# A token MLP in which every product reads the two halves of its columns in turn

## The chip, the cores and the metric

The kernel runs on one core of one Trainium2 chip. The metric is the device time of one execution in microseconds. Three executions of the kernel before gave 1683.47, 1689.55 and 1690.23 us; their median, 1689.55 us, is the number that a changed kernel is held against.

## The reference

Two stages. The first is a long convolution along the sequence, with a filter made from a small MLP of position embeddings; the second is an MLP over all 24,960 tokens.

```python
def _attn_ref(x, v, pos_emb, w1, w2):            # x, v: 2 x 12480 x 128
    h_filt = (np.maximum(pos_emb @ w1, 0.0) @ w2) * np.exp(-0.01 * pos)[:, None]
    u = x * v
    y = irfft(rfft(u, n=2 * S) * rfft(h_filt, n=2 * S)[None])[:, :S]   # along the sequence
    return x * y

def _moe_ref(x, w_in, w_out):                    # x: 24960 x 128, w_in: 128 x 2048
    h = x @ w_in
    return np.maximum(0.01 * h, h) @ w_out       # w_out: 2048 x 128
```

## The kernel before, in words

The convolution is done as matrix products with the factors of a transform, in four steps with two trips through DRAM. Batch 0 goes through its first three steps ahead of the MLP; batch 1 and the last step of both run inside the MLP's loop, cut into pieces by hand.

The MLP holds tokens along the columns. The 24,960 columns are cut into 50 tiles: one of 390, 46 of 512, one of 314 and two of 352 (`widths`). For each tile k and each of 16 slices f of the 2048 hidden channels, `m1(k, f)` makes 128 hidden channels and `m2(k, f, r)` adds their share to the output. Numbers are split into a high and a low part of the type float32r (`zh`, `zl` for the input; `rh`, `rl` for the hidden values; `w_in_h`, `w_in_l`, `w_out_h`, `w_out_l` for the weights), and each product is three matmuls, high by high, high by low, low by high. In each of them the 128x128 piece of the weights stands in the array, and the tile of `zh`, `zl`, `rh` or `rl`, up to 512 columns long, moves through it. So a step (k, f) is six matmuls: three into a PSUM tile `mh` (line 977), three that add to the PSUM tile `acc` of the tile k (lines 1010 to 1012).

Between the two, the hidden values are taken out of `mh`. There are two ways. Where `sums(k)` holds (21 of the 50 tiles, all in the first half), ScalarE writes `rh` as the positive part of `mh` (line 981) and VectorE writes `rl` as what is left of it, reading `mh` too (line 982); the linear part of the activation then enters through three extra matmuls per tile with a product matrix `wc` (lines 1006 to 1008). In the other 29 tiles ScalarE reads `mh` once and writes `r` (line 990), and `rh` and `rl` are made from `r` in SBUF: `rh` by ScalarE for even f (line 994), by VectorE for odd f (line 992), `rl` by VectorE (line 995).

The order is written out by hand in the last loop of the kernel: `m1` of a step, then `m2` of the step three steps before (`DEEP` is 3), then whatever pieces of convolution, loads and the output stage are due at that step. `mh` has three PSUM buffers, `rh` and `rl` have five SBUF buffers each, and there are two `acc` tiles, used in turn.

When a tile is done, `finish(k)` copies `acc` to SBUF tiles `ot` of 390 columns each (line 1025, ScalarE); TensorE transposes each `ot`, and it goes out.

Of the kernel before, what the change touches and what calls it, by code (L numbers as in the profile page):

```python
# [12 lines left out]
AF = mybir.ActivationFunctionType  # L13
ALU = mybir.AluOpType
# [16 lines left out]
def tile_conv_mlp(ctx, tc, x, v, pos_emb, w1, w2, w_in, w_out, cf, cr, cg, cb, ci, cw, out):  # L31
    nc = tc.nc
# [78 lines left out]
    def run(g):  # L111
        for _ in g:
            pass


    def chunk(c):
        k0 = c * KC
        return k0, min(KC, NA - k0)
# [36 lines left out]
    def back(dp, parts, c):  # L155

        for s in range(2):
            for j, w in halves(c):
                three(dp[s][:, w], (mi_h[j][:, s], mi_l[j][:, s]), (parts[0][:, s, w], parts[1][:, s, w]))

    def turned(pool, psum, m2, m1):

        ph = pool.tile([128, 2, KH + 1], F32, tag="ph0", name="ph0", bufs=1)
# [50 lines left out]
    with tc.manual_schedule():  # L214
# [22 lines left out]
        with ExitStack() as st:  # L237
# [86 lines left out]
            for c in range(NC0):  # L324
# [52 lines left out]
                for mm in range(MC):  # L377
                    a = psa.tile([NA, 2, 512], F32, tag="a", name="a", bufs=3)
# [193 lines left out]
        ld, cin, z, acc = {}, {}, {}, {}  # L572
# [103 lines left out]
        with ExitStack() as st:  # L676
# [73 lines left out]
            def two(tag):  # L750
                return [psb.tile([128, 512], F32, tag=tag, name=tag + "p", bufs=2) for _ in range(2)]
# [41 lines left out]
            for i, c in enumerate(ORD):  # L793
# [16 lines left out]
                n = chunk(c)[1]  # L810
                t, es = bins.pop(c), eh.pop(c)
                hp = two("h")
                for ri in range(2):
                    for k in range(n):
                        h, j = 64 * (k % 2), ri * n // 2 + k // 2
# [53 lines left out]
        widths = [TOK] + [WIDE] * ((S - TOK) // WIDE) + [rest]  # L869
# [9 lines left out]
        def sums(k):  # L879
            return at0[k] < S and k not in OWN and k < LAST  # L880

        def pieces_of(t):

            for k in range(NTL):
                lo, hi = max(at0[k], t * TOK), min(at0[k + 1], t * TOK + TOK)
                if lo < hi:
                    yield k, lo - at0[k], lo - t * TOK, hi - lo
# [81 lines left out]

        def m1(k, f):  # L970
            w = widths[k]
            zh, zl = (i[:, :w] for i in z[k])
            hp = ps.tile([128, WIDE], F32, tag="mh", name="mh", bufs=3)[:, :w]
            fs = slice(f * 128, f * 128 + 128)
            for i, (u, m) in enumerate(((w_in_h, zh), (w_in_l, zh), (w_in_h, zl)) if k == f == 0 else
                                       ((w_in_h, zh), (w_in_h, zl), (w_in_l, zh))):
                nc.tensor.matmul(hp, u[:, fs], m, start=(i == 0), stop=(i == 2))  # L977
            rh = sm.tile([128, WIDE], F32R, tag="rh", name="rh", bufs=DEEP + 2)[:, :w]
            rl = sm.tile([128, WIDE], F32R, tag="rl", name="rl", bufs=DEEP + 2)[:, :w]
            if sums(k):  # L980
                nc.scalar.activation(out=rh, in_=hp, func=AF.Relu)  # L981
                nc.vector.scalar_tensor_tensor(out=rl, in0=hp, scalar=0.0, in1=rh, op0=ALU.max, op1=ALU.subtract)  # L982
            else:
                tag, pool, bufs = ((("th", psc["pool"], 1), ("tl", psc["pool"], 1), ("ct1", psc["pool"], 1),
                                    ("ph", psc["pool"], 1), ("pl", psc["pool"], 1)) if k in OWN else
                                   (("s1", s0, 3), ("hd", psc["pool"], 2), ("ct1", psc["pool"], 1),
                                    ("s1", s0, 3), ("hd", psc["pool"], 2)))[f % 5]
                r = pool.tile([128, 2048 if tag == "hd" else 1024], F32R if tag in ("th", "tl", "ph", "pl") else F32,
                              tag=tag, name="r", bufs=bufs)[:, :w].bitcast(F32)
                nc.scalar.activation(out=r, in_=hp, func=AF.Lrelu, alpha=0.01)  # L990
                if f % 2:
                    nc.vector.tensor_copy(rh, r)  # L992
                else:
                    nc.scalar.copy(rh, r)  # L994
                nc.vector.tensor_tensor(out=rl, in0=r, in1=rh, op=ALU.subtract)  # L995
            return rh, rl

        def m2(k, f, r):
            rh, rl = r
            w = widths[k]  # L1000
            if f == 0:
                acc[k] = ps.tile([128, WIDE], F32, tag=f"acc{k % 2}", name="acc", bufs=1)
            if f == 0 and sums(k):
                zh, zl = (i[:, :w] for i in z[k])
                ap = acc[k][:, :w]
                nc.tensor.matmul(ap, wc_h, zh, start=True, stop=False)
                nc.tensor.matmul(ap, wc_h, zl, start=False, stop=False)
                nc.tensor.matmul(ap, wc_l, zh, start=False, stop=False)
            ap = acc[k][:, :w]
            nc.tensor.matmul(ap, w_out_h[:, f, :], rh, start=(f == 0 and not sums(k)), stop=False)  # L1010
            nc.tensor.matmul(ap, w_out_h[:, f, :], rl, start=False, stop=False)  # L1011
            nc.tensor.matmul(ap, w_out_l[:, f, :], rh, start=False, stop=(f == NF - 1))  # L1012

        ots = {}

        def finish(k):

            ap = acc.pop(k)
            whole = []
            for t in range(at0[k] // TOK, (at0[k + 1] - 1) // TOK + 1):  # L1020
                for kk, a, c, n in pieces_of(t):
                    if kk == k:
                        if t not in ots:
                            ots[t] = sm.tile([128, TOK], F32, tag="ot", name="ot", bufs=3)
                        nc.scalar.copy(ots[t][:, c:c + n], ap[:, a:a + n])
                        if c + n == TOK:
                            whole.append(t)
            for t in whole:
                yield
                b, mp = divmod(t, NT)  # L1030
                ot = ots.pop(t)
                end = t == total - 1
                op = ps.tile([NA, 4, D], F32, tag="io", name="op")
                op0 = ps.tile([128, WIDE], F32, tag="cv", name="op0", bufs=2)[:NA].rearrange(
                    "a (q d) -> a q d", d=D) if end else op
                for p, m, at, n in COLS:
                    nc.tensor.transpose((op if p else op0)[:, 2 * p + m, :], ot[:, at:at + NA], ident)  # L1037
                os_ = sm.tile([NA, 2, 2, D], F32, tag="os", name="os")
                n = b * S
                dst = out[n:n + ROWS * NB, :].rearrange("(a p n) d -> a p n d", p=2, n=HB)  # L1040
                r0 = n + ROWS * NB + 2 * mp
                if end:
                    nc.scalar.copy(os_[:, 1], op[:, 2:4])
                    nc.vector.tensor_copy(os_[:, 0], op0[:, 0:2])
                    for eng, p in ((nc.scalar, 1), (nc.sync, 0)):
                        eng.dma_start(out=dst[:R0, p, 2 * mp:2 * mp + 2, :], in_=os_[:R0, p])
                    nc.scalar.dma_start(out=dst[R0:, :, 2 * mp:2 * mp + 2, :], in_=os_[R0:ROWS])
                    nc.sync.dma_start(out=out[None, r0:r0 + 2, :], in_=os_[ROWS:, 0])
                    return
                nc.scalar.copy(os_.rearrange("a p m d -> a (p m) d"), op)  # L1050
                yield
                for r in (slice(0, R0), slice(R0, ROWS)):
                    nc.sync.dma_start(out=dst[r, :, 2 * mp:2 * mp + 2, :], in_=os_[r])
                nc.sync.dma_start(out=out[None, r0:r0 + 2, :], in_=os_[ROWS:, 0])
# [34 lines left out]
        for t in range(1, total):  # L1089
            g, p = turn_at[t], turn_at.get(t - 1, 0)  # L1090
            if t in leads:
                lo = max(g - 19, p + 2, gets[t] + 7)
                till = ends[t - 1] if t - 1 in second and g - ends[t - 1] < 8 else g - 2
                hi = max((lo + till) // 2, gets[t + 1] + 7)
# [3 lines left out]
            elif t in gets and t not in second:  # L1098
                lo = max(g - 9, p + 1, gets[t] + 5)
# [85 lines left out]
        for k in range(NTL):  # L1185
            for f in range(NF):
                i = k * NF + f
                pend.append((k, f, m1(k, f)))
                if len(pend) > DEEP:
                    m2(*pend.pop(0))  # L1190
                for s_ in steps.get(i, ()):
                    do(*s_, i)
                if f == DEEP - 1 and k:
                    fin = finish(k - 1)
                if f >= DEEP - 1 and (f - DEEP + 1) % 2 == 0:
                    next(fin, None)
                if i < SLOTS:
                    while done < min(pieces, pace(i)):
                        next(conv, None)
                        done += 1  # L1200
        for q in pend:
            m2(*q)
        run(finish(NTL - 1))


# [66 lines left out]
```

## Time and profile before

| what | us |
|---|---|
| median of three runs | 1689.55 |
| the profiled execution, its own time | 1684.68 |
| its span, first to last instruction | 1682.9 |
| TensorE busy within the span | 1628.1 |
| VectorE busy | 1193.9 |
| ScalarE busy | 1008.0 |
| GpSimd busy | 821.6 |

The profile is of one execution. A busy time says how long an engine had an instruction in work; it is an average over stages. Matmuls overlap at their ends, so the time that a matmul takes on its row is longer than the distance from its start to the start of the next, and it is the distance that counts for the sum. The MLP begins at 337 us and runs to the end.

### The profile page before, as it was taken

Reading aid. Unit: us, or ns where it says so; the run is one execution under the profiler, and the core shown is the slowest. Engines: PE = TensorE matmul, PEld = TensorE weight load, DVE = VectorE, ACT = ScalarE, POOL = GpSimd, SP = SyncE. Lnnn points to the kernel's source line nnn. Section 1 sums busy time; section 2 is a strip of 40 time slices with the busy share of each in tenths; the row PEclk is TensorE's granted clock in tenths of the full one; section 3 lists DMA queues with packets and bytes.
Section 4 is the critical chain, followed back from the end, with each engine's and each line's share of the span. In section 5 each row is a group of like instructions: output and inputs, shape, how many; then the busy total and the mean of one; then the engine's idle time right before and its main releaser. Section 6 shows DMA issues by size and latency. Waiting matters only on the chain.

```text
span 1682.9 us, 27337 instructions
## 1 busy us (share of the span) xinstructions
PE 1628.1 (97%) x9173; PEld 1319.2 (78%) x9173; DVE 1193.9 (71%) x1785; ACT 1008.0 (60%) x2056; POOL 821.6 (49%) x804
## 2 busy tenths in 40 slices
PE   6897999899999999999999999999999999999999
PEld 6786555488888888888888888888888888887888
DVE  4775888656775566666566664887887887878765
ACT  1332454345654577676677676666667676676666
POOL 3563212245643376767567763654464545445410
PEclk9998999999999999999999999999999999999999
DMA  8898999766766466656566631321212212121100
GB/s 237 285 301 248 342 321 342 253 195 186 209 177 196 124 170 196 192 157 171 155 177 165 167 105 55 122 68 56 61 61 66 75 53 75 56 61 56 56 11 20
DMA packets 166357, 253.30 MB, mean 151 GB/s; under 512 B 14302, under 2 KB 119026, under 8 KB 163146
## 3 DMA queue, kind: packets, MB, share of 16 engines
q1 hardware_dynamic: 146478, 226.29, 45.6%
q10 hardware_dynamic: 19740, 25.28, 4.3%
q8 instruction: 73, 1.20, 0.3%
q14 instruction: 66, 0.54, 0.1%
HBM read 168.00 MB, written 83.43 MB: 149 GB/s over the span
## 4 chain that ended last, share of the span: by engine, by line
PE 79%; DVE 9%; DMA 7%; issue 2%; ACT 1%; SPq 1%; POOL 0%; ACTq 0%; DVEq 0%; POOLq 0%
PE mh L977 30%; PE acc L1011 10%; PE acc L1012 10%; PE acc L1010 10%; PE cv L138 4%; PE yp L903 4%; PE cv L425 3%; DMA scr<-o 2%; DMA ft<-in_cf_dram 2%; PE op L1037 2%; PE zp L922 1%; PE up L124 1%; DVE rl L995 1%; DVE ta L132 1%; PE a L381 1%
## 5 line engine op out<-in xcount | busy, mean ns | idle before, releaser
L995 DVE TENSOR_TENSOR rl<-r,rh 128x512 fp32r<-128x512 f32 (+2 forms) x464 | 398.1, 875 | 101.0 <-ACT rh L994 92.4
L990 ACT ACTIVATE r<-mh 128x512 f32<-128x512 f32 (+2 forms) x464 | 271.3, 586 | 193.8 <-PE mh L977 175.2
L982 DVE SCALAR_TENSOR_TENSOR rl<-mh,rh 128x512 fp32r<-128x512 f32 (+1 forms) x336 | 227.8, 683 | 222.9 <-ACT rh L981 220.6
L977 PE MATMUL mh<-zh,w_in_h 128*128 128x512 f32 (+3 forms) x800 | 327.6, 410 | 0.8 <-ACT zh L966 0.7
L1011 PE MATMUL acc<-rl,w_out_h 128*128 128x512 f32 (+3 forms) x800 | 309.6, 387 | 1.3 <-DVE rl L995 0.6
L977 PE MATMUL mh<-zh,w_in_l 128*128 128x512 f32 (+3 forms) x800 | 310.3, 388 | 0.0
L1010 PE MATMUL acc<-rh,w_out_h 128*128 128x512 f32 (+3 forms) x800 | 310.3, 388 | 0.0
L1012 PE MATMUL acc<-rh,w_out_l 128*128 128x512 f32 (+3 forms) x800 | 309.9, 387 | 0.0
L977 PE MATMUL mh<-zl,w_in_h 128*128 128x512 f32 (+3 forms) x800 | 309.4, 387 | 0.0
L981 ACT ACTIVATE rh<-mh 128x512 fp32r<-128x512 f32 (+1 forms) x336 | 199.7, 596 | 157.3 <-PE mh L977 151.4
L936 POOL TENSOR_TENSOR zl<-zf,zh 128x390 fp32r<-128x390 f32 (+24 forms) x110 | 69.3, 643 | 406.1 <-ACT zh L935 401.0
L666 POOL TENSOR_TENSOR cp<-cq,cp 98x256 f32<-98x256 f32 x248 | 223.0, 899 | 34.4 <-DVE cp L654 17.7
L992 DVE CAST rh<-r 128x512 fp32r<-128x512 f32 (+2 forms) x232 | 146.5, 632 | 48.6 <-ACT r L990 47.3
L1011 PEld LDWEIGHTS acc<-rl,w_out_h 128*128 128x128 f32 x800 | 150.3, 188 | 38.5 <-DVE rl L995 7.0
L977 PEld LDWEIGHTS mh<-zh,w_in_l 128*128 128x128 f32 x800 | 150.7, 188 | 32.1
L977 PEld LDWEIGHTS mh<-zh,w_in_h 128*128 128x128 f32 x800 | 151.2, 189 | 31.1 <-issue 3.9
L1012 PEld LDWEIGHTS acc<-rh,w_out_l 128*128 128x128 f32 x800 | 150.3, 188 | 30.7
L1010 PEld LDWEIGHTS acc<-rh,w_out_h 128*128 128x128 f32 x800 | 150.4, 188 | 30.2
L977 PEld LDWEIGHTS mh<-zl,w_in_h 128*128 128x128 f32 x800 | 151.5, 189 | 24.1 <-DVE zl L968 0.2
L994 ACT CAST rh<-r 128x512 fp32r<-128x512 f32 (+2 forms) x232 | 140.9, 607 | 7.3
L663 POOL TENSOR_TENSOR cq<-cin 98x256 f32<-98x256 f32 x124 | 120.1, 968 | 0.8 <-DMA cin<-scr 0.8
L654 POOL TENSOR_TENSOR cp<-cin 98x256 f32<-98x256 f32 x78 | 74.6, 975 | 66.3 <-PE yp L903 32.0
(165 smaller groups left out, 2390.1 us busy)
## 6 DMA issues: line engine op xcount, KB each, us to landing
cin<-scr SPq DMA_DIRECT2D x318, 98.0 KB
hd<-hspec SPq DMA_DIRECT2D x48, 512.0 KB
bin<-scr SPq DMA_DIRECT2D x23, 768.0 KB
scr<-o SPq DMA_DIRECT2D x28, 588.0 KB
scr<-ct SPq DMA_DIRECT2D x25, 512.0 KB
scr1b<-o SPq DMA_DIRECT2D x32, 392.0 KB
hspec<-hs ACTq DMA_DIRECT2D x48, 256.0 KB
xm<-in_x_dram SPq DMA_DIRECT2D x128, 96.0 KB
```

Source lines behind the costliest of these rows:

```text
L663: eng.tensor_tensor(out=cq[:, p], in0=ci_t[:, 0, :, 0, :], in1=ci_t[:, 0, :, 1, :], op=op)
L666: eng.tensor_tensor(out=cp[:, p, w], in0=cq[:, p], in1=cp[:, p, 1], op=op)
L977: nc.tensor.matmul(hp, u[:, fs], m, start=(i == 0), stop=(i == 2))
L981: nc.scalar.activation(out=rh, in_=hp, func=AF.Relu)
L982: nc.vector.scalar_tensor_tensor(out=rl, in0=hp, scalar=0.0, in1=rh, op0=ALU.max, op1=ALU.subtract)
L990: nc.scalar.activation(out=r, in_=hp, func=AF.Lrelu, alpha=0.01)
L992: nc.vector.tensor_copy(rh, r)
L994: nc.scalar.copy(rh, r)
L995: nc.vector.tensor_tensor(out=rl, in0=r, in1=rh, op=ALU.subtract)
L1010: nc.tensor.matmul(ap, w_out_h[:, f, :], rh, start=(f == 0 and not sums(k)), stop=False)
L1011: nc.tensor.matmul(ap, w_out_h[:, f, :], rl, start=False, stop=False)
L1012: nc.tensor.matmul(ap, w_out_l[:, f, :], rh, start=False, stop=(f == NF - 1))
```

## The change

The columns of a moving operand are no longer read in order. With a width w, the matmul reads column 0, then column w/2, then 1, then w/2 + 1, and so on: two runs, one column of each in turn. In a tile of 512 columns each step goes 256 columns, 1024 bytes, forwards or back. The product therefore lands in PSUM with its columns in that mixed order, in a contiguous run of PSUM as before. Those who read `mh` or `acc` undo it: they read PSUM with a step of two, first the even places and then the odd ones, and write SBUF in the plain order. All data in SBUF stays where it was.

```diff
+    def mixed(t):
+        return t.rearrange("p (h i) -> p i h", h=2)
+    def plain(t):
+        return t.rearrange("p (i h) -> p h i", h=2)
+    def split2(t):
+        return t.rearrange("p (h i) -> p h i", h=2)
...
         def m1(k, f):
-            zh, zl = (i[:, :w] for i in z[k])
+            zh, zl = (mixed(i[:, :w]) for i in z[k])
...
-                nc.scalar.activation(out=rh, in_=hp, func=AF.Relu)
-                nc.vector.scalar_tensor_tensor(out=rl, in0=hp, scalar=0.0, in1=rh, op0=ALU.max, op1=ALU.subtract)
+                nc.scalar.activation(out=split2(rh), in_=plain(hp), func=AF.Relu)
+                nc.vector.scalar_tensor_tensor(out=split2(rl), in0=plain(hp), scalar=0.0, in1=split2(rh),
+                                               op0=ALU.max, op1=ALU.subtract)
...
-                nc.scalar.activation(out=r, in_=hp, func=AF.Lrelu, alpha=0.01)
+                nc.scalar.activation(out=split2(r), in_=plain(hp), func=AF.Lrelu, alpha=0.01)
...
         def m2(k, f, r):
-            rh, rl = r
+            rh, rl = (mixed(i) for i in r)
...
-                zh, zl = (i[:, :w] for i in z[k])
+                zh, zl = (mixed(i[:, :w]) for i in z[k])
...
-                        nc.scalar.copy(ots[t][:, c:c + n], ap[:, a:a + n])
+                        half = widths[k] // 2
+                        for h in range(2):
+                            lo, hi = max(a, half * h), min(a + n, half * h + half)
+                            if lo < hi:
+                                nc.scalar.copy(ots[t][:, c + lo - a:c + hi - a],
+                                               plain(ap[:, :2 * half])[:, h, lo - half * h:hi - half * h])
```

The order of instructions on TensorE, VectorE, GpSimd and the DMA queues is the same in both kernels, with the same sizes. On ScalarE, a copy of `acc` to `ot` that lies across the middle of its tile becomes two: 111 copies become 161, of the same 24,960 columns. Below is ScalarE at the end of one tile of 512, before (`os` is a finished output tile, `cv` a PSUM tile of the convolution):

```order
L990 ACTIVATE r<-mh 128x512
L105 COPY a1s<-cv 98x512
L981 ACTIVATE rh<-mh 128x512 x3
L1025 COPY ot<-acc 128x24
L1025 COPY ot<-acc 128x390
L1025 COPY ot<-acc 128x98
L981 ACTIVATE rh<-mh 128x512
```

and the same place on ScalarE after the change:

```order
L1003 ACTIVATE r<-mh 128x512
L105 COPY a1s<-cv 98x512
L993 ACTIVATE rh<-mh 128x512 x3
L1042 COPY ot<-acc 128x24
L1042 COPY ot<-acc 128x232
L1042 COPY ot<-acc 128x158
L1042 COPY ot<-acc 128x98
L993 ACTIVATE rh<-mh 128x512
```

The copy of 390 columns is now one of 232 and one of 158; nothing else moved.

## Rows read from the trace of the kernel before

**Rows 1.** The page: busy time by engine; TensorE and its clock in 40 slices.
```profile
PE 1628.1 (97%) x9173; PEld 1319.2 (78%) x9173; DVE 1193.9 (71%) x1785; ACT 1008.0 (60%) x2056; POOL 821.6 (49%) x804
...
PE   6897999899999999999999999999999999999999
...
PEclk9998999999999999999999999999999999999999
```

**Rows 2.** Two stretches: length; busy us of PE, PEld, DVE, ACT, POOL; clock; DMA.
```profile
1100.00:1600.00 500.00, 499.32 (x2575) 405.85 (x2574) 406.33 (x513) 344.91 (x686) 251.38 (x268) 1.00 0.20 61
600.00:1000.00 400.00, 399.95 (x2005) 325.21 (x2005) 261.17 (x356) 280.44 (x569) 284.42 (x272) 1.00 0.62 171
```

**Rows 3.** TensorE in order of time, steady: start, us, line, shape.
```profile
900.00 0.39 PE L977 MATMUL mh<-zh,w_in_h 128*128 128x512 f32 x1
...
901.37 0.39 PE L138 MATMUL cv<-ph,mi_h 128*128 128x512 f32 x1
...
1639.81 0.40 PE L977 MATMUL mh<-zl,w_in_h 128*128 128x512 f32 x1
...
1642.84 0.40 PE L977 MATMUL mh<-zh,w_in_l 128*128 128x512 f32 x1
...
1659.70 0.32 PE L977 MATMUL mh<-zh,w_in_h 128*128 128x352 f32 x1
...
1662.90 0.32 PE L977 MATMUL mh<-zh,w_in_l 128*128 128x352 f32 x1
```

**Rows 4.** TensorE at the start of the MLP, and that stretch's clock (0.64).
```profile
338.49 0.53 PE L977 MATMUL mh<-zh,w_in_h 128*128 128x390 f32 x1
...
340.12 0.53 PE L977 MATMUL mh<-zh,w_in_l 128*128 128x390 f32 x1
...
347.17 0.34 PE L977 MATMUL mh<-zl,w_in_h 128*128 128x390 f32 x1
...
350.00 0.34 PE L1012 MATMUL acc<-rh,w_out_l 128*128 128x390 f32 x1
...
337.00:342.00 5.00, 4.72 (x18) 4.50 (x19) 3.80 (x9) 2.22 (x6) 0.17 (x1) 0.64 0.56 184
```

**Rows 5.** Groups by line and shape, TensorE's weight loads: busy us, mean ns.
```profile
L977 PEld LDWEIGHTS mh<-zl,w_in_h 128*128 128x128 f32 x800 | 151.5, 189 | 24.1 <-DVE zl L968 0.2
L903 PEld LDWEIGHTS yp<-cp,gt 98*64 98x64 f32 x1008 | 54.9, 138 | 13.3 <-issue 10.5 <-DVE cp L666 1.0 <-ACT zh L935 0.7
L124 PEld LDWEIGHTS up<-bin,mb 128*64 128x64 f32 x200 | 13.2, 140 | 21.4 <-issue 11.3 <-PE hp L816 4.3 <-DVE tb L132 4.2
```

**Rows 6.** The same view of ScalarE and VectorE, 128 rows or 98, by shape.
```profile
L990 ACT ACTIVATE r<-mh 128x512 f32<-128x512 f32 x416 | 249.6, 601 | 181.4 <-PE mh L977 163.2 <-DVE rl L995 2.3
L990 ACT ACTIVATE r<-mh 128x352 f32<-128x352 f32 x32 | 15.0, 468 | 7.7 <-PE mh L977 7.7
L1025 ACT COPY ot<-acc 128x390 f32<-128x390 f32 x17 | 8.4, 492 | 0.0
L1025 ACT COPY ot<-acc 128x290 f32<-128x290 f32 x2 | 0.8, 400 | 0.0
L995 DVE TENSOR_TENSOR rl<-r,rh 128x512 fp32r<-128x512 f32 x416 | 370.8, 910 | 89.7 <-ACT rh L994 81.8
L982 DVE SCALAR_TENSOR_TENSOR rl<-mh,rh 128x512 fp32r<-128x512 f32 x320 | 218.9, 689 | 215.6 <-ACT rh L981 213.4
L107 DVE TENSOR_TENSOR o<-cv,a1s 98x512 f32<-98x512 f32 x29 | 19.8, 682 | 0.0
L107 DVE TENSOR_TENSOR o<-a,a1s 98x384 f32<-98x384 f32 x64 | 35.2, 550 | 34.8 <-DMA scr<-o 24.8 <-ACT a1s L105 7.4 <-ACT pts L293 2.1
L87 DVE TENSOR_SCALAR fa<-wi 128x256 uint32<-128x256 uint32 x8 | 2.3, 283 | 0.3 <-DMA wo<-in_moe_w_out_dram 0.3
L88 DVE TENSOR_SCALAR fb<-fa 128x256 uint32<-128x256 uint32 x16 | 4.7, 294 | 0.6
```

## The prediction

> **What bounds the kernel now.** I read the busy times and the slices first [rows 1]: TensorE is busy 97% of the span and at nine tenths or more in nearly every slice from the start of the MLP at 337 us, at the full clock of 2.4 GHz. Then two long stretches, one in each half of the MLP [rows 2]: TensorE is busy 399.95 of 400 us and 499.32 of 500, the next busiest engine 280 and 406. So TensorE alone sets the end, and the others have slack: ScalarE 120 of 400 us and 155 of 500, VectorE 139 and 94. The last thing to read is the pace of the matmuls, start to start [rows 3]: six steps from 900.00 to 901.37 are 228 ns each, thirteen from 1639.81 to 1642.84 are 233 ns; I take 230.7 ns for 512 columns. For 352 columns it is twenty steps in 3.20 us, 160 ns. The difference of 71 ns for 160 columns is 0.44 ns a column. So a matmul is a stream of columns at close to one for each cycle of the 2.4 GHz clock (0.417 ns), with about 15 ns around it.
>
> **What the change does, part by part.** Four edits.
>
> First, the moving operand of every MLP matmul. The matmuls, their number, widths and order stay; what differs is where the next column lies: beside the last one before, 1 KB away now. How many columns: 24,960 tokens by 16 slices by 6 matmuls are 2,396,160, and the `wc` products of 21 tiles (one of 390, twenty of 512) add three times 10,630, so 2,428,050 in all. What they cost today: 4,476 matmuls of 512 at 230.7 ns are 1032.6 us; 99 of 390 at 177 ns (sixteen steps from 347.17 to 350.00 [rows 4]) 17.5; 192 of 352 at 160 ns 30.7; 96 of 314 at 145 ns (by proportion) 13.9. Together 1094.7 us of the span, all on the path that sets the end.
>
> No row of this trace has a moving operand that jumps at every column, so the price has to be bounded. From below: the weight load of `yp` (line 903) takes every second column of its tile, and its 64 columns take 138 ns against 140 ns for 64 adjacent ones of line 124 [rows 5]. On VectorE, line 87 reads every second word and takes 283 ns for 256 columns, line 88 reads adjacent ones and takes 294 [rows 6]. By these a jump is free. They are jumps of two words, though, not of 256. From above: what 4-byte columns cost other readers that take them one at a time. TensorE's own weight loads: 189 ns for 128 columns and 140 for 64, 0.77 ns a column [rows 5]. ScalarE: 601 ns for 512 and 468 for 352, 0.83 ns [rows 6]. VectorE: 682 for 512 and 550 for 384, 1.03 ns [rows 6]. Only the moving operand, with its columns side by side, goes at 0.44. And there is a row for this very product at half that speed: at the start of the MLP, on the lower clock of 1.2 GHz, five matmuls of 390 from 338.49 to 340.12 are 326 ns each [rows 4], 0.833 ns a column and nothing around it.
>
> I take 0.833 ns: one column for each cycle of the lower clock level, which lies between the weight loads and VectorE, and is a pace at which this stream is seen to run. The argument is that a stream of 0.44 ns a column is faster than every other reader of 4-byte columns in this trace, so it must be taking more than one column per access, and a jump at each column takes just that away. 2,428,050 columns at 0.833 ns are 2023.4 us, 928.7 more than today. At 0.75 ns it would be 726 more, at 1.03 ns 1406.
>
> The Trainium skill (Advanced Engine Details and Errata, section SBUF Cachelines) speaks against the change: lines in SBUF are 16 bytes, and accesses that each go to another line pay a penalty, since it takes at least two hits on one line to absorb the latency. It gives no figure for TensorE. The rows with steps of 8 bytes have two words in each such line, so their being free does not contradict it; the sum above would stand as it is.
>
> Second, ScalarE and VectorE read `mh` with a step of two. By lines 87 and 88 that is free; from above, a second column time for every column: 0.83 ns by 512 is 427 ns more on line 990 or 981 (601 ns), 1.03 by 512 is 527 more on line 982 (689 ns). Even then ScalarE would be busy 345 + 325 x 0.427 = 484 us in the stretch of 500, which would itself be three quarters longer by the first edit (1950 matmuls by 197 ns). So in the likeliest case it is hidden at either price. Without that cover see the second rival.
>
> Third, 50 more copies `ot`. Two rows of line 1025, 492 ns for 390 and 400 for 290, put what a copy costs beside its columns at some 130 ns: 50 of them are 7 us of ScalarE over 1340, in its slack. TensorE does not wait for them at once: `acc` alternates between two tiles.
>
> Fourth, nothing moves in the queues: TensorE, VectorE, GpSimd and DMA have the same rows in the same order, and no wait for another engine's result is added in the loop. Weight loads of 189 ns still fit under a matmul of 427. The 337 us ahead of the MLP are untouched.
>
> The sum: 1682.9 + 928.7 = 2611.6 us of span, 1.8 us around it as before (1684.68 against 1682.9), and 4.9 us because the median of the runs stands that much above the profiled one: 2618 us. The bounds 0.75 and 1.03 ns give 2416 and 3096.
>
> **The rivals.** One: the reader keeps both runs. Each of the two runs moves on by one column at a time, so whatever was fetched with a column of the first half may still be held when its neighbour is asked for two columns later. Then the stream stays at 0.44 ns, the other edits lie in the slack, and the time is 1690 us: not slower. For it: the free steps of two in lines 903 and 87. Against it: those never leave a short neighbourhood. The point from which it decides is whether a column costs below 0.46 ns.
>
> Two: TensorE keeps its pace, and the step of two in PSUM is what costs. In the second half ScalarE has 155 us of slack for 325 reads of `mh` [rows 2], 0.48 us each; at 427 ns more it stays within, with waits that bunch, some 1 to 2%: 1700 to 1720. At two more column times (854 ns) ScalarE would need 345 + 277 = 622 us for 500, and in the first half VectorE 261 + 214 x 1.05 = 487 for 400: about 1.23 times the 1340 us of the MLP, 2000. I put it at 1800, between the two.
>
> Three: a jump costs more than one cycle of the lower clock. The row for it, at some distance, is line 995, where VectorE with two operands from SBUF takes 910 ns for 512 columns, 1.78 ns each [rows 6]. That would be 4322 us for the columns, 4920 in all.
>
> Both the first and the third have something behind them in the Trainium skill (Vector Engine (DVE) Microarchitecture Reference, section 5.2 on measured stream behaviour): on VectorE a source that jumps 4 KiB at every element costs 1.73 ns a column against 1.05, which as an estimate from that page, carried over to TensorE, would be 4810 us here; but a single stream that alternated between two regions 16 KiB apart ran at the full rate there, which would be 1690. No run here shows either.
>
> Four: a price between 0.46 and 0.75 ns a column, as when pairs of accesses overlap in part: 1740 to 2416.
>
> **How the numbers follow.** Forecast (2416 to 3096) 0.45, since the argument from the readers' paces needs only that adjacency is what makes the stream fast. Rival one 0.17: the pattern is as regular as a jump can be. Rival two 0.09, since it needs the first edit to be free as well. Rival three 0.17. Rival four 0.09. The last 0.03 are for a stream that gets faster: at most the 15 ns around each matmul, which are absent on the lower clock, 4,863 by 15 ns, 73 us. About 0.5% is what a measurement of this kernel can tell from no change. Slower: 0.45 + 0.09 + 0.17 + 0.09 = 0.80; same 0.17; faster 0.03. The range from 1680 to 3100 holds rivals one, two and four and the forecast, 0.80; it leaves out rival three. The forecast's own range is 2416 to 3096.
>
> **What would show it.** Right: from 340 us on, matmuls of 512 columns start 427 ns apart at the full clock, TensorE is still busy without gaps, ScalarE and VectorE fall to about half their share, and the part ahead of 337 us is unchanged. Rival one: starts 228 to 233 ns apart, and a span as before. Rival two: the same pace within a group of six, but gaps ahead of lines 1010 and 1011 of the old numbering that end with ScalarE's `rh` or VectorE's `rl`, and line 990 well above 601 ns. Rival three: starts 0.9 us apart. The prediction is wrong if the pace lies outside 0.39 to 0.53 us.

## The result, and the profile after

The changed kernel takes 1638.51 us (median of four runs, 1635.82 to 1639.52) against 1687.64 us for the kernel before: a ratio of 0.9716, 95% interval 0.9699 to 0.9734. I had forecast 2618 us. It is 49 us faster instead of 930 slower.

The page of the profile after, busy times and TensorE's slices (compare [rows 1]):

```profile
span 1636.2 us, 27293 instructions
...
PE 1574.4 (96%) x9173; PEld 1320.3 (81%) x9173; DVE 1186.6 (73%) x1785; ACT 1010.4 (62%) x2106; POOL 818.0 (50%) x804
...
PE   7897999899999999999999999999999999999999
...
PEclk9899999989999999999999999999999999999999
```

The two stretches of [rows 2] after the change (length; busy us of PE, PEld, DVE, ACT, POOL with counts; clock; DMA share; GB/s):

```profile
600.00:1000.00 400.00, 397.81 (x2087) 338.05 (x2086) 268.28 (x366) 289.09 (x602) 287.96 (x275) 1.00 0.60 168
...
1100.00:1600.00 500.00, 495.26 (x2661) 420.79 (x2660) 409.78 (x534) 361.42 (x736) 238.04 (x257) 1.00 0.19 59
```

In the same 500 us TensorE now gets through 2661 matmuls where it was 2575, yet it is idle for 4.7 us where it was idle for 0.7. Both matter below. The pace itself, TensorE in order of time (start, us on its row, line, shape; line 989 is what was line 977), as in [rows 3]:

```profile
450.79 0.38 PE L989 MATMUL mh<-zl,w_in_h 128*128 128x512 f32 x1
...
452.95 0.38 PE L1025 MATMUL acc<-rh,w_out_l 128*128 128x512 f32 x1
...
1604.87 0.31 PE L989 MATMUL mh<-zl,w_in_h 128*128 128x352 f32 x1
...
1608.00 0.31 PE L1024 MATMUL acc<-rl,w_out_h 128*128 128x352 f32 x1
```

Ten steps in 2.16 us are 216 ns for 512 columns, where it was 228 to 233; 21 steps in 3.13 us are 149 ns for 352, where it was 160. At 2.4 GHz 512 columns are 213.3 ns and 352 are 146.7. The stream now goes at one column a cycle with under 3 ns around a matmul. And the readers of PSUM, groups by line and shape (busy us, mean ns), as in [rows 6]:

```profile
L1003 ACT ACTIVATE r<-mh 128x512 f32<-128x512 f32 x416 | 249.0, 600 | 152.6 <-PE mh L989 134.7 <-DVE rl L1008 7.8 <-DVE zt L925 3.5
...
L994 DVE SCALAR_TENSOR_TENSOR rl<-mh,rh 128x512 fp32r<-128x512 f32 x320 | 218.0, 688 | 197.1 <-ACT rh L993 196.2
```

600 and 688 ns where it was 601 and 689: reading PSUM with a step of two costs ScalarE and VectorE nothing.

### The profile page after: what moved, and what is told of

Read it like the earlier page. It is cut to its first block, busy times and chain, and to the rows that moved or that the text cites. A ratio compares the mean times of both kernels' runs of the same rounds, so it can differ in the third digit from the quotient of the medians.

```text
span 1636.2 us, 27293 instructions
## 1 busy us (share of the span) xinstructions
PE 1574.4 (96%) x9173; PEld 1320.3 (81%) x9173; DVE 1186.6 (73%) x1785; ACT 1010.4 (62%) x2106; POOL 818.0 (50%) x804
## 3 DMA queue, kind: packets, MB, share of 16 engines
q1 hardware_dynamic: 146478, 226.29, 46.7%
## 4 chain that ended last, share of the span: by engine, by line
PE 63%; DVE 12%; DMA 11%; ACT 5%; issue 5%; POOL 2%; SPq 1%; ACTq 0%; DVEq 0%; POOLq 0%
PE mh L989 23%; PE acc L1024 8%; PE acc L1025 7%; PE acc L1023 7%; DVE rl L1008 5%; PE yp L915 4%; PE cv L150 3%; DVE rh L1005 3%; PE cv L437 3%; DMA scr<-ct 2%; DMA ft<-in_cf_dram 2%; DMA scr<-o 1%; PE op L1055 1%; PE zp L934 1%; PE up L136 1%
## 5 line engine op out<-in xcount | busy, mean ns | idle before, releaser
L989 PE MATMUL mh<-zh,w_in_h 128*128 128x512 f32 (+3 forms) x800 | 316.9, 396 | 2.7 <-DVE rl L994 1.5
L1024 PE MATMUL acc<-rl,w_out_h 128*128 128x512 f32 (+3 forms) x800 | 304.4, 380 | 6.8 <-DVE rl L1008 6.3
L989 PE MATMUL mh<-zl,w_in_h 128*128 128x512 f32 (+3 forms) x800 | 300.0, 375 | 0.1
L989 PE MATMUL mh<-zh,w_in_l 128*128 128x512 f32 (+3 forms) x800 | 299.8, 375 | 0.0
L1025 PE MATMUL acc<-rh,w_out_l 128*128 128x512 f32 (+3 forms) x800 | 299.2, 374 | 0.0
L1023 PE MATMUL acc<-rh,w_out_h 128*128 128x512 f32 (+3 forms) x800 | 299.2, 374 | 0.0
```

## Experiments

### Where does the gain sit: one part of the change at a time

**e2_hidden_only.** Halves in turn only for the three matmuls into `mh`:

```diff
-            rh, rl = (mixed(i) for i in r)
+            rh, rl = r
...
-                zh, zl = (mixed(i[:, :w]) for i in z[k])      # the wc products in m2
+                zh, zl = (i[:, :w] for i in z[k])
```

and `finish` copies `acc` in plain order again.

> Only the three matmuls into mh read halves in turn; those into acc read in order. If the gain is 15 ns in each matmul that reads in turn, half of it is left: 24 us below the kernel before, 1664. If the gain came from the input tiles zh and zl alone: 1640. If it came from rh and rl alone: 1688.

Measured: 1663.34 us, ratio 0.9869 (0.9845 to 0.9893).

**e3_out_only.** The opposite: `m1` and its readers as in the kernel before, halves in turn for all matmuls into `acc`.

> Only the matmuls into acc (with the wc products) read halves in turn; those into mh read in order. If each matmul gains 15 ns: half of the gain, 1664 us. If the input tiles alone gave it: 1688; if rh and rl alone: 1640.

Measured: 1662.44 us, ratio 0.9865 (0.9839 to 0.989). Each half of the change gives half of the gain, so it belongs to each matmul that reads in turn and not to one operand.

**e4_readers_only.** All matmuls in plain order; ScalarE and VectorE still read PSUM with a step of two. The columns of the result are then not in their places.

```diff
-            zh, zl = (mixed(i[:, :w]) for i in z[k])
+            zh, zl = (i[:, :w] for i in z[k])
...
-            rh, rl = (mixed(i) for i in r)
+            rh, rl = r
```

> All matmuls read in order as before, and ScalarE and VectorE read PSUM with a step of two (the columns of the result then stand in another order than the reference's). If the gain is in the moving operand: as the kernel before, 1686 to 1690 us, matmuls 228 to 233 ns apart, line 1003 at 600 ns. If reading PSUM with a step of two takes a conflict off TensorE's writes: 1640 us.

Measured: 1686.55 us, ratio 1.0 (0.9987 to 1.0014). The readers have no part in it, neither as a cost nor as a gain.

### What a stream of columns costs, measured by itself

**e1_bench.** The kernel before, with groups of test matmuls behind its end; each group is a loop of this form, with another access pattern for the moving operand:

```diff
         run(finish(NTL - 1))
+        for j in range(18):
+            if j % 3 == 0:
+                pt = ps.tile([128, WIDE], F32, tag="mh", name="pt", bufs=3)
+            nc.tensor.matmul(pt, w_out_h[:, j % NF, :], w_in_h[:, 1024:1536].rearrange("p (h i) -> p i h", h=2),
+                             start=(j % 3 == 0), stop=(j % 3 == 2))
```

> The kernel before with a row of test matmuls behind its last step (the result is made as before; the time of the whole says nothing). Each group is 18 matmuls (24, 30 or 72 in some) of 512 columns in float32r with weights of 128 columns, from start to start. Theory A, the stall is in the plain stream itself: 228 to 233 ns for plain order with every other engine idle, 215 to 216 for two halves in turn. Theory B, it comes from the weight load that runs under the matmul: plain order 228 with weights of 128 columns, about 222 with 64 and below 219 with 32. Theory C, it comes from the other engines' or the transfers' traffic in SBUF: 215 to 216 for plain order while they are idle, and 228 or more only in the groups beside VectorE, ScalarE, GpSimd or transfers. Runs of 2, 4, 8 and more columns from each half, and jumps of 2 to 128 columns, tell how near or far a jump must be: if a 16-byte stretch counts, jumps of 2 stay at 228 and jumps of 4 and more go to 215.5; if a larger bank counts, only far jumps do. 16-bit operands in plain order: 215.5 in every theory that rests on bytes per column. If jumps cost anywhere as I had forecast, some group stands at 400 ns or more.

One line of the program is one group: its count, its shortest, median and longest row in ns, and its first and last start in us, which divided by the count less one give the distance. In this order: plain order, two halves in turn, four quarters in turn, eight eighths; plain again, pairs of columns from each half; then the columns of every four read as 0 2 1 3, and of every eight as 0 4 1 5 2 6 3 7; plain order with weights of 32 columns; then 16-bit operands, plain order and halves in turn. Last the window in which most of them ran: its length, then the busy us of TensorE, of its weight loads, and of VectorE, ScalarE and GpSimd.

```profile
L1220 PE MATMUL pt<-w_in_h,w_out_h x18: 389/389/389, 1696.7 to 1700.5; 128*128 128x512 f32 x18
L1225 PE MATMUL pt<-w_in_h,w_out_h x18: 378/379/379, 1700.8 to 1704.4; 128*128 128x512 f32 x18
L1230 PE MATMUL pt<-w_in_h,w_out_h x18: 436/451/451, 1704.6 to 1709.4; 128*128 128x512 f32 x18
L1235 PE MATMUL pt<-w_in_h,w_out_h x18: 667/667/724, 1709.7 to 1718.1; 128*128 128x512 f32 x18
L1265 PE MATMUL pt<-w_in_h,w_out_h x18: 389/389/415, 1758.3 to 1762.2; 128*128 128x512 f32 x18
L1270 PE MATMUL pt<-w_in_h,w_out_h x18: 496/513/513, 1762.4 to 1768.2; 128*128 128x512 f32 x18
L1305 PE MATMUL pt<-w_in_h,w_out_h x18: 389/389/389, 1794.2 to 1798.0; 128*128 128x512 f32 x18
L1310 PE MATMUL pt<-w_in_h,w_out_h x18: 378/379/379, 1798.3 to 1801.9; 128*128 128x512 f32 x18
L1360 PE MATMUL pt<-w_in_h,w_out_h x18: 390/394/398, 1838.3 to 1842.2; 128*32 128x512 f32 x18
L1420 PE MATMUL pt<-hb x18: 378/379/380, 1901.2 to 1904.9; 128*128 128x512 bf16 x18
L1425 PE MATMUL pt<-hb x18: 645/646/647, 1905.1 to 1913.3; 128*128 128x512 bf16 x18
1696.70:1833.00 136.30, 136.30 (x483) 92.90 (x482) 0.00 (x0) 0.00 (x0) 0.00 (x0) 1.00 0.00 0
```

With every other engine and all transfers idle, plain order still takes 224 to 229 ns and halves in turn 212 to 218 (starts are given to 0.1 us here, so a group of 18 is good to some 6 ns). That rules out the other engines' traffic as the source of this difference, and the groups run beside a busy VectorE, ScalarE, GpSimd or transfers are no different, 227.6 to 228 ns in plain order and 214 to 217 in turn, but for one group whose first matmul waited. Weights of 32 columns leave plain order at 229, so the weight load has no part in it either. The loss is in the plain stream itself. Of the two patterns with near jumps 0 2 1 3 stays at 224 ns, and 0 4 1 5 2 6 3 7 has the whole gain, 212. But not every jump is free: four runs in turn take 282 ns, eight 494, pairs from each half 341, and 16-bit operands lose from halves in turn, 218 to 482. What I had forecast for the change, 427 ns, is near what 8 to 256 runs in turn cost here, 435 to 494.

The same test was made at other widths. Below are the groups in order of time: start, length of the whole group of 18 in us, line, shape; at each width plain order first and halves in turn behind it.

```profile
1696.67 4.24 PE L1220 MATMUL pt<-w_in_h,w_out_h 128*128 128x512 f32 x18
1700.75 4.05 PE L1225 MATMUL pt<-w_in_h,w_out_h 128*128 128x512 f32 x18
...
1854.49 3.06 PE L1390 MATMUL pt<-w_in_h,w_out_h 128*128 128x352 f32 x18
1857.40 2.85 PE L1395 MATMUL pt<-w_in_h,w_out_h 128*128 128x352 f32 x18
1860.08 3.38 PE L1400 MATMUL pt<-w_in_h,w_out_h 128*128 128x390 f32 x18
1863.29 3.18 PE L1405 MATMUL pt<-w_in_h,w_out_h 128*128 128x390 f32 x18
```

Plain order loses 0.19 us in 18 matmuls of 512 columns, 0.20 in 18 of 390 and 0.21 in 18 of 352: 11 to 12 ns a matmul at every width. The loss does not grow with the columns; in proportion to them it would be 0.13 us at 352. At 352 that is also what a matmul gains in the loaded kernel, 11 ns. At 512 it gains 15 there, and where the other 4 come from, no run shows.

**e5_streams.** The same, with groups of 48 and with patterns chosen to tell what is counted. Here a stream is a pair (start, step), and two streams in turn supply the even and the odd places of the moving operand.

> The kernel before with groups of 48 test matmuls behind its last step, nothing else running (the time of the whole says nothing). Theory two readers: columns at even places and columns at odd places of the moving operand are fetched by two readers, each of which keeps the stretch of four adjacent columns that it is in; it is the two being in one stretch that costs the plain order its 13 to 15 ns. Then two streams whose second lies 4 or more columns on run at 215 ns, with 0 to 3 columns on at 223 to 229; two streams of step 2 lose something (each fetch serves two columns), of step 4 they fall to 430 or more (each fetch serves one); the first column of each half, then the second of each, is 215 and pairs from each half 341 (as in e1_bench), though both touch the same stretches at the same time; step 2 is about 450. Rival kept stretches: TensorE keeps the last two stretches whoever asked; then pairs from each half, and two streams of step 2, would run at 215 too, and only patterns with three or more open stretches are slow. One column for all: 215 in both, if it is fetches that cost; 228 if the plain order's loss has nothing to do with where columns lie.

The same view; in this order: plain order; halves; two streams of step 1, the second 0, 3 and 4 columns on; two streams of step 2, 3 and 4, 1024 columns apart; one stream of step 2, of step 3; pairs from each half; the first column of each half and then the second of each; four quarters.

```profile
L1217 PE MATMUL pt<-w_in_h,w_out_h x48: 389/389/389, 1698.5 to 1709.1; 128*128 128x512 f32 x48
L1222 PE MATMUL pt<-w_in_h,w_out_h x48: 378/379/379, 1709.3 to 1719.5; 128*128 128x512 f32 x48
L1227 PE MATMUL pt<-w_in_h,w_out_h x48: 379/379/379, 1719.7 to 1729.8; 128*128 128x512 f32 x48
L1242 PE MATMUL pt<-w_in_h,w_out_h x48: 379/379/382, 1750.8 to 1761.0; 128*128 128x512 f32 x48
L1247 PE MATMUL pt<-w_in_h,w_out_h x48: 379/379/379, 1761.2 to 1771.3; 128*128 128x512 f32 x48
L1317 PE MATMUL pt<-w_in_h,w_out_h x48: 389/389/395, 1906.6 to 1917.2; 128*128 128x512 f32 x48
L1322 PE MATMUL pt<-w_in_h,w_out_h x48: 502/514/514, 1917.5 to 1933.4; 128*128 128x512 f32 x48
L1327 PE MATMUL pt<-w_in_h,w_out_h x48: 625/632/634, 1933.8 to 1955.0; 128*128 128x512 f32 x48
L1332 PE MATMUL pt<-w_in_h,w_out_h x48: 632/632/632, 1955.4 to 1976.6; 128*128 128x512 f32 x48
L1337 PE MATMUL pt<-w_in_h,w_out_h x48: 630/633/635, 1977.1 to 1998.2; 128*128 128x512 f32 x48
L1357 PE MATMUL pt<-w_in_h,w_out_h x48: 498/502/515, 2041.5 to 2057.2; 128*128 128x512 f32 x48
L1362 PE MATMUL pt<-w_in_h,w_out_h x48: 378/379/385, 2057.5 to 2067.7; 128*128 128x512 f32 x48
L1372 PE MATMUL pt<-w_in_h,w_out_h x48: 437/438/442, 2081.9 to 2094.7; 128*128 128x512 f32 x48
```

In ns from start to start, good to some 2 ns: plain 225.5; halves 217; two streams of step 1 215 to 217, whatever lies between them, even nothing; two of step 2 225.5, of step 3 338, of step 4 451; one stream of step 2 451, of step 3 449; pairs 334; first of each, then second of each 217; quarters 272. One column for all, which is not in the list, takes 217.

One part of my theory fell: two streams in the same stretch of four columns at once (0 or 3 columns on) cost nothing, so that is not what plain order loses by. What stands is simpler. Sort the columns by place, even and odd, 256 each. In plain order each of the two goes on by two columns at a time, and two streams of step 2 that lie 1024 columns apart take the same time. Then 451, 338 and 225.5 ns for steps of 4, 3 and 2 are 256, 192 and 128 times 1.76 ns: one fetch of 1.76 ns for each new stretch of four columns that a side enters. At a step of 1 it would be 64 fetches, 113 ns, and the stream's own 213 ns is the longer. One stream of step 2 or 3 gives each side a step of 4 or 6, a new stretch every time: 451 and 449. The rival, that TensorE keeps the last two stretches whoever asked, falls with the pairs: they touch the same stretches as "first of each, then second of each" and take 334 against 217.

That there really are two readers by place is a model that fits these steps at 512 columns, not something a row shows; and it doesn't give everything. With quarters or pairs each side goes to and fro between two stretches, and takes 272 and 334, between the 225 and less of a side that keeps both and the 451 of one that keeps one. Pieces of 4 to 32 columns from each half enter no more stretches than plain order and take 253 to 241 ns in e1_bench; plain order from one or two columns further on takes 235 there. And for 352 and 390 columns the count gives 155 and 172 ns, where the groups of e1_bench in plain order (3.06 and 3.38 us less a last row of 0.32 and 0.34, over 17) take 161 and 179. So the step of each side decides between gain and loss; what plain order loses its 11 to 12 ns by stays open.

### The same in the whole kernel

**e7_quarters.** The changed kernel with four quarters in turn in the tiles of 512 and 352:

```diff
+    def runs(t):
+        return 4 if t.shape[1] % 4 == 0 else 2
...
-        return t.rearrange("p (h i) -> p i h", h=2)
+        return t.rearrange("p (h i) -> p i h", h=runs(t))
```

and the same in `plain`, `split2` and `finish`.

> The changed kernel with four quarters of the columns in turn instead of two halves, in all tiles whose width is a multiple of four (of 512 and 352); ScalarE and VectorE read PSUM with a step of four. If it is two streams that run free and more do not (282 ns per 512 in e1_bench): 4476 x 66 ns and some 9 us for the tiles of 352, 300 us above the changed kernel, 1930 to 1960. If any regular pattern runs free in the loaded kernel: 1640. If it costs as my forecast had it (0.833 ns a column): 2560 or more.

Measured: 1886.48 us, ratio 1.118 (1.1158 to 1.1202). Matmuls of 512 are 273 ns apart. 57 ns more than halves, times 4,476, is 255 us, which puts it at 1894. My expectation had used the 282 ns of e1_bench; the same pattern takes 272 in e5_streams, and why the two differ is open. TensorE in order of time:

```profile
899.57 0.44 PE L993 MATMUL mh<-zh,w_in_h 128*128 128x512 f32 x1
...
901.21 0.60 PE L1060 MATMUL op<-ident,ot 128*98 128x128 f32 x4
```

**e9_near.** Two runs only four columns apart. The readers are those of the kernel before, so the columns of the result are not in their places; the same holds for the next kernel.

```diff
+    def mixed(t):
+        if t.shape[1] % 8:
+            return t.rearrange("p (h i) -> p i h", h=2)
+        return t.rearrange("p (g h i) -> p g i h", h=2, i=4)
```

`m1` and `m2` use it in the places in which the change uses its own `mixed`.

> All MLP matmuls read in turn as in the changed kernel, but from two runs only 4 columns apart: 0 4 1 5 2 6 3 7, then the next eight (the tiles of 390 and 314, no multiples of eight, read their halves). ScalarE and VectorE read and write in plain order as in the kernel before, so the columns of the result stand in another order than the reference's. Theory, from e5_streams: what counts is that the columns at even places, and those at odd places, each go on by one column at a time, so that a 16-byte stretch is fetched once for four of them; then distance is nothing: 1638 us, ratio 0.970 to 0.973. Rival, the two runs must lie far apart, in other parts of SBUF: 1688.

Measured: 1637.67 us, ratio 0.9718 (0.9687 to 0.9749), the whole gain.

**e10_every_second.** The same two halves in turn, but every second column of each first:

```diff
+    def mixed(t):
+        if t.shape[1] % 4:
+            return t.rearrange("p (h i) -> p i h", h=2)
+        return t.rearrange("p (h i l) -> p l i h", h=2, l=2)
```

> All MLP matmuls read their two halves in turn, one column of each, 256 apart as in the changed kernel, but take every second column of each half first and the others after: 0 256 2 258 ..., then 1 257 3 259 ... (the tiles of 390 and 314 as in the changed kernel); ScalarE and VectorE as in the kernel before, so the columns of the result stand in another order. Theory: the columns at even places now go on by two, as in plain order, so twice the fetches: 225 to 232 ns a matmul and the time of the kernel before, 1680 to 1690, ratio 0.995 to 1.00. Rival, alternating between two halves is what gives the gain: 1638, ratio 0.9716.

Measured: 1683.62 us, ratio 0.9988 (0.9975 to 1.0002), none of the gain. TensorE in order of time:

```profile
901.25 0.39 PE L982 MATMUL mh<-zh,w_in_h 128*128 128x512 f32 x1
...
903.08 0.39 PE L982 MATMUL mh<-zh,w_in_l 128*128 128x512 f32 x1
```

Eight steps in 1.83 us, 229 ns. These two are the test that I trust most: in the one the halves have gone and the gain stays, in the other the halves stay and the gain has gone. It is the step of each side that counts.

### Where the rest of the gain went

At 216 in place of 230.7 ns for 4,476 matmuls, 149 in place of 160 for 192, and some 10 ns less for each of the 195 others, TensorE would save 66 + 2 + 2 = 70 us by my estimate (58 with 228 ns in place of 230.7, 80 with 233). The span fell by 46.7. TensorE's weight loads, what they waited for (us in total, times, longest), before and then after:

```profile
PEld acc L1011 <- DVE rl L995: 7.0, 15, 0.7
```

```profile
PEld acc L1024 <- DVE rl L1008: 24.0, 51, 0.9
...
PEld mh L989 <- DVE rl L994: 7.4, 16, 0.9
```

The second of these was 2.6 us before. So TensorE's weight loads wait some 22 us more for VectorE's `rl`. Not all of that is lost time: in the stretch of 500 us TensorE's own idle time rose by 4 us. TensorE has become fast enough to catch up with VectorE in the second half of the MLP, where VectorE is the busier of the two helpers (410 of 500 us, ScalarE 361). The same wait of line 1024 is 14.7 us in e2_hidden_only and 13.6 in e3_out_only, which may be why each of them gave half of the 49 us and not half of the 70.

**e6_shift.** The changed kernel, with an eighth of the casts to `rh` (two slices of 16) moved from VectorE to ScalarE:

```diff
-                if f % 2:
+                if f % 2 and f % 8 != 7:
                     nc.vector.tensor_copy(rh, r)
```

> The changed kernel, and in the tiles that make rh from r, the cast of f 7 and 15 goes from VectorE to ScalarE (58 casts; in the second half about 28 us of VectorE's 410 in 500). If what keeps the gain below 4863 matmuls by 15 ns is that TensorE now waits for VectorE's rl: 4 to 10 us below the changed kernel, ratio 0.966 to 0.969 to the kernel before. If those waits are bunching that a cast less does not touch: 0.9716 as the changed kernel. If ScalarE becomes late instead: 0.974 or more.

Measured: 1627.68 us, ratio 0.9655 (0.9634 to 0.9677): 11 us below the changed kernel, a little more than I had expected. The wait that was 24.0 us is 7.1:

```profile
PEld acc L1024 <- DVE rl L1008: 7.1, 16, 0.7
```

So 17 us less of waiting gave 11 us of time. Some 10 us of the estimated 70 are still missing, which is within the doubt about the 70.

**e11_shift_alone.** The same edit in the kernel before.

> The kernel before, in plain order, with the casts of f 7 and 15 given to ScalarE as in e6_shift. If that is worth something only because the changed kernel made TensorE wait for VectorE: the waits of TensorE's weight loads for rl are 7 us in the kernel before, so 0 to 5 us less, ratio 0.997 to 1.00. If the shift is worth 11 us by itself: 0.9935.

Measured: 1683.72 us, ratio 0.9989 (0.9973 to 1.0006), no more than 5 us and perhaps nothing. The shift pays only with the faster matmuls.

**e8_all_in_turn.** e6_shift, and the float32r products of the convolution inside the MLP also read halves in turn:

```diff
-                        three(up[s][:, :w].rearrange("p (k d) -> p k d", d=D), (mb_h[:, s], mb_l[:, s]),
-                              (th[:, :n, s, :], tl[:, :n, s, :]))
+                        three(up[s][:, :w].rearrange("p (k d h) -> p k d h", d=D, h=2), (mb_h[:, s], mb_l[:, s]),
+                              [i[:, :n, s, :].rearrange("p (h k) d -> p k d h", h=2) for i in (th, tl)])
```

and likewise for `back`, with a step of two for their readers.

> e6_shift, and the float32r products of the convolution inside the MLP (line 150 of the changed kernel, 300 matmuls of up to 512 columns) also read halves in turn, with a step of two in PSUM for their readers. If a matmul in plain order loses 15 ns wherever it stands: 300 x 15 ns, 4 us below e6_shift, a ratio lower by 0.003. If the loss belongs to the MLP's operands: no difference.

Measured: 1624.59 us, ratio 0.9621 (0.9602 to 0.964). It is the fastest of all. That it is 3 us below e6_shift agrees with 300 matmuls by some 15 ns, but the two intervals overlap, so the times alone do not show it. The rows do. Six such matmuls in a row (line 150 in both), in e6_shift and then here:

```profile
894.83 0.40 PE L150 MATMUL cv<-th,mb_h 128*128 128x512 f32 x1
...
896.00 0.40 PE L150 MATMUL cv<-th,mb_l 128*128 128x512 f32 x1
```

```profile
893.51 0.38 PE L150 MATMUL cv<-th,mb_h 128*128 128x512 f32 x1
...
894.59 0.38 PE L150 MATMUL cv<-th,mb_l 128*128 128x512 f32 x1
```

Five steps in 1.17 us are 234 ns, five in 1.08 are 216. The loss is not one of the MLP's operands alone.

## Why the prediction was wrong

**The step that failed** is the price of the moving operand: "a stream of 0.44 ns a column is faster than every other reader of 4-byte columns in this trace, so it must be taking more than one column per access, and a jump at each column takes just that away". The first half agrees with e5_streams. The second does not hold: a jump at each column takes nothing away when what is jumped between are two streams that each go on by one. The price is 216 ns for 512 columns, 0.42 ns a column. The price that I took, 0.833 ns a column (427 ns), does exist nearby: one stream of step 2 takes 451 ns. I had priced jumps in general, and the change makes a special one.

**The bounds** were wrong on the lower side too. I let the price go down to that of today's stream and took what today's stream has beyond 0.417 ns a column, "about 15 ns around it", for something that stays. That it lies around the matmul and not in its columns agrees with e1_bench, where plain order loses 11 to 12 ns at 512, 390 and 352 columns alike. That it stays was never asked. The row on the lower clock, 326 ns for 390 columns at 1.2 GHz, which alone are 325 [rows 4], shows that not every such matmul pays it. The prediction even had the sum, at most 73 us of gain. It gave this case no mechanism, only the last 0.03, and left it out of both ranges: 1638.51 us lies below 1680.

**Rival one** had the right mechanism and the wrong size: each run goes on by one column and is not lost between two visits, as I wrote; but I let the stream "stay at 0.44 ns" there, where it falls to 0.42. The Trainium skill (Vector Engine (DVE) Microarchitecture Reference, section 5.2) has a stream that alternates between two far regions at every element at full rate on VectorE; the halves in turn agree for TensorE, at 216 ns for 512 columns. I had set that observation beside the dearer one, 1.73 ns a column, without asking what sets the two apart. (The sum from 1.73 ns a column comes to 4795 us and not to 4810, without effect on the forecast.)

**The Trainium skill's rule on SBUF lines** (Advanced Engine Details and Errata, section SBUF Cachelines) speaks of 16 bytes and of two hits needed per line. The runs agree on the 16 bytes, four columns of four bytes: steps of 3 cost three quarters of steps of 4. But in plain order each side of the model has its two hits, and 512 columns still take 12 ns more than the stream's 213; and in the changed kernel each access does go to another line than the one before it, without a penalty.

**The other edits** went as told. The step of two in PSUM is free (600 and 688 ns; e4_readers_only 1.0), the 50 more copies are hidden, and the start of the MLP stands at 338.29 us where it was 337.27. What I did not see is what a faster TensorE brings to light, the waiting for VectorE, worth 11 us in e6_shift: I had looked for waits only in the case where TensorE gets slower or the readers do.

## What to carry to other kernels

Don't take for given what a matmul takes beyond its columns. Here 11 to 15 ns of it hung on the order in which the columns are read; that it is absent on the lower clock was one sign, and a few test matmuls behind the kernel showed it. For float32r moving operands that bind, read two runs in turn, each by one column at a time, near or far, and let the readers of PSUM put the order right with a step of two. Don't take it further (four runs, pairs, 16-bit operands, one stream of step 2 all lost here), and look at once at which engine now feeds TensorE too late.

## What the runs showed of the hardware

- A float32r matmul of 512 columns in plain order at 2.4 GHz takes 225.5 to 228 ns from start to start with everything else idle, 228 to 233 in the loaded kernel; with two runs in turn 215 to 217 in both. With everything else idle the loss of plain order is 11 to 12 ns at 512, 390 and 352 columns (e1_bench).
- At 512 columns its time agrees with the larger of 0.417 ns a column and 1.76 ns for each new stretch of four columns that the even or the odd places enter: 225.5, 338 and 451 ns for steps of 2, 3 and 4 on each side. It does not agree for four runs, for pairs, for pieces of 4 to 32 columns, or at 352 and 390 columns.
- For other operands the same pattern is a loss: 16-bit operands go from 218 to 482 ns (e1_bench), and plain float32, whose matmuls have two rows each, from 429 to 540 ns a row:

```profile
L1410 PE MATMUL pt<-w_in_h,w_out_h x36: 591/592/592, 1866.3 to 1881.3; 128*128 128x512 f32 x36
...
L1415 PE MATMUL pt<-w_in_h,w_out_h x36: 701/703/705, 1881.8 to 1900.7; 128*128 128x512 f32 x36
```
